# A written order for VectorE, ScalarE and TensorE in the opening of a float32 attention and GEGLU kernel, without waits between neighbours

## The chip, the cores and the metric

The kernel runs on one core of one Trainium2 chip. The metric is device time in microseconds (us) of one execution. One profiled execution gives the span, the instructions of each engine, their waits and the DMA transfers; its own device time stands beside its span below.

## The reference

All tensors are float32. From the same x (2048 tokens, 512 channels) two branches are computed and mixed by a gate for each token:

```python
x = A_x
g = _sigmoid((x * gate_w).sum(-1, keepdims=True))
a = _A_ref(x, A_wqkv, A_wo)
b = _B_ref(x, B_w_gate, B_w_up, B_w_down)
return g * a + (1 - g) * b
```

Branch A is attention with 32 heads of 16 channels. Each token looks at itself and at the seven tokens 2, 4, ... 14 places before it, then comes the product with wo. Branch B is `(gelu(x @ w_gate) * (x @ w_up)) @ w_down` with 1792 hidden channels.

## The kernel before

**Precision.** TensorE reads fp32r, a rounded float32. So each operand is split into a high part (`hi`, the rounded value, made by a ScalarE activation `AF.Copy`) and a low part (`lo = raw - hi`, made by a VectorE subtraction). A product of two operands is three matmuls: hi x hi, lo x hi, hi x lo. The helper `split` (line 81) issues both, hi first.

**Two halves of tokens.** Tokens are worked on in two halves (`par` 0 and 1) of 1024, each as eight tiles of 128 (`jj`), four to a block. Each half has a projection to K and Q, one to V and the gate, an FFN of 14 chunks (`ffn`, `gate_up`, `down`) and four units of attention on VectorE (`scores`, `softmax`, `mix`), spread between the matmuls of the FFN by `pull`. A scheduler sorts what the program leaves open, from priorities and an estimate of times; the result is a fixed sequence of instructions for each engine.

**The opening** is `start()` (from line 834 on). It makes K and Q of the first half, as a 2 x 2 block product in seven block products (Strassen's scheme in Winograd's form) in place of eight. The operands are a11, a12, a21, a22 of x (512 tokens or channels each) and b11, b12, b21, b22 of the weights, and their sums:

- x: s1 = a21 + a22, s2 = s1 - a11, s4 = a12 - s2, s3 = a11 - a21. In the code `q[kc][0..3]` are a11, a12, a21, a22 of one K chunk (kc 0 or 1), and `s12` holds s1 and then s2.
- weights, in place: t1 = b12 - b11, t2 = b22 - t1, t3 = b22 - b12, t4 = b21 - t2.

`block(ps, a, w, ...)` issues the 24 matmuls of one block product: four tiles, two K chunks, three matmuls each. The order is a11 x b11 (into the banks `U`, acc0 to acc3), a12 x b21 (into `V_`, four banks of tag p, seeded with a copy of U), s1 x t1 (`Z_`, the same four banks again), s2 x t2 (onto U), s4 x b22 (onto Z_), s3 x t3 (onto U), a22 x t4 (onto U). Between them ScalarE evicts: `put` writes K and Q of the first two units from V_ and in the end from U, `p5` is the copy of Z_ after s1 x t1, `u2` that of U after s2 x t2. `join` adds such a copy to a bank on VectorE and stores K and Q of the other two units over SP's queue.

The first half block (tile 0 of a11 x b11) runs on the first 128 tokens that land. Then come two fillers, and the first chunk for the other three tiles.

**What sets the order.** `row` (class `Row`, line 815) wraps VectorE: each instruction that it issues gets a dependency of class Sync on the one before, so a semaphore wait on its predecessor. `mm` and the fillers are chained through `paced` and `LAST` in the same way on TensorE. ScalarE has no written order in the opening; the scheduler places its roundings and evictions. SP's queue carries the loads, in the order that the scheduler gives it: x, weights, then the stores of K and Q, the loads of the FFN (`fetch`, `fetch_d`) and of the V weights (`vs`).

**Where tiles come free.** `RAW` (the FFN weights of a chunk) takes the two `raw` tiles that hold x, `XR`, so chunk 0 and 1 are loaded when the last low part has been read from them. The V weights' raw tiles are four of tag c, two of which held parts of b22 and t3. The weights b11, b21, b12 and b22 lie in the tiles `prod`, `v` and `tb` that attention uses later.

**After the opening**: `sums(f)` forms the four sums of the FFN weights of a chunk (the FFN uses the same seven products, line 497), `parts(i)` splits them into the tiles g0 and g1, and `ffn(0)` starts with the V projection of tile 0 and 1 among its products (line 189).

Of the kernel before, what the change touches and what calls it, by code (L numbers as in the profile page):

```python
# [37 lines left out]
BT = 4  # L38
# [9 lines left out]
def tile_gated_mix(ctx: ExitStack, tc: tile.TileContext, xt, wqkv, wff, wo, out):  # L48
# [308 lines left out]
    def after(ins, other):  # L357

        tc.add_manual_dep(ins.ins, other.ins.name, mybir.DependencyInfo(mybir.DependencyClass.Sync,
                          mybir.DependencyReason.SCHED_ONLY), reason="pace")  # L360

    def paced(ins):
        after(ins, LAST[-1])
# [452 lines left out]
    class Row:  # L816

        last = None

        def __getattr__(self, name):  # L820
            def do(*args, **kw):
                ins = getattr(nc.vector, name)(*args, **kw)
                if Row.last is not None:
                    after(ins, Row.last)
                Row.last = ins
                return ins
            return do

    row = Row()
# [5 lines left out]
    def start():  # L835
# [5 lines left out]
        for kc in range(2):  # L841
            XR[kc] = tl("raw")

# [7 lines left out]
        def quarters(t):  # L851
            return [t[:, i * 512:(i + 1) * 512] for i in range(4)]

        def operand(name, src, rooms_):
            KW[name] = [tuple(rooms_[2 * k:2 * k + 2]) for k in range(2)]
            for k in range(2):
                split(row, *KW[name][k], src[:, k * 512:(k + 1) * 512])
# [3 lines left out]

        def rooms_of(tag, n, w=512):
            t = tl(tag, F32R)
            return [t[:, i * w:i * w + 512] for i in range(n)]
# [15 lines left out]
        KW["b11"] = [tuple(g1a[2 * k:2 * k + 2]) for k in range(2)]  # L880
        split_x(0, 0, 0, ((0, P),), row.tensor_copy, row)
        split(row, *KW["b11"][0], b11[:, :512])
        split_x(0, 0, 0, ((P, 512 - P),), row.tensor_copy, row)
        split_x(0, 0, 1, eng=row)
        split(row, *KW["b11"][1], b11[:, 512:])
        U = [bank(f"acc{t}") for t in range(BT)]

        def mm(ps, t, a, w, first=False, last=False):
            ins = nc.tensor.matmul(ps, a[:, t * P:(t + 1) * P], w, start=first, stop=last, skip_group_check=True)  # L889
            paced(ins)  # L890
            LAST[:] = [ins]

        (xh, xl), (wh, wl) = X[0, 0, 0], KW["b11"][0]
# [3 lines left out]
        for _ in range(FILLERS):  # L897
            ins = nc.tensor.matmul(U[-1][:, :P], warm[:, :P], warm[:, :P], start=True, stop=True)
            paced(ins)
            LAST[:] = [ins]  # L900
# [6 lines left out]
        def block(ps, a, w, first, then, kcs=(0, 1)):  # L907
            for t in range(BT):
                for kc in kcs:
                    ah, al = XOP[a, kc]  # L910
                    wh, wl = KW[w][kc]
                    for n, (a_, w_) in enumerate(((ah, wh), (al, wh), (ah, wl))):
                        mm(ps[t], t, a_, w_, first and kc == 0 and n == 0, kc == 1 and n == 2)
                if then:
                    then(t)

        for n, blk, k in (("a11", 0, 0), ("a12", 0, 2), ("a22", 1, 2)):
            for kc in range(2):
                XOP[n, kc] = X[0, blk, kc + k]
        V_ = []  # L920

        def seed(t):
            V_.append(bank("p"))
            nc.scalar.activation(V_[t], U[t], AF.Copy)

        block(U, "a11", "b11", False, seed, (1,))
        split_x(0, 0, 2, eng=row)
        split_x(0, 0, 3, eng=row)
        operand("b21", b21, g1b)

        def put(jj, ps):
            take_first(ps, jj, lambda o, i: nc.scalar.activation(o, i, AF.Copy))

        block(V_, "a12", "b21", False, lambda t: put(t, V_[t]))
# [7 lines left out]
        q = [quarters(XR[kc]) for kc in range(2)]  # L942
# [3 lines left out]
        for kc in range(2):  # L946
# [5 lines left out]
        p5, u2 = [], []  # L952

        def keep_p5(t):
            p5.append(tl("hh")[:, :512])
            nc.scalar.activation(p5[t], Z_[t], AF.Copy)

        def keep_u2(t):
            u2.append(tl("hl")[:, :512])
            nc.scalar.activation(u2[t], U[t], AF.Copy)  # L960
# [7 lines left out]
        block(Z_, "s1", "t1", True, keep_p5)  # L968
        for kc in range(2):
            sub(s12[kc], s12[kc], q[kc][0])  # L970
        for kc in range(2):
            split(row, *XOP["s2", kc], s12[kc])
        sub(b11, b22, b11)
        operand("t2", b11, d[4:])
        block(U, "s2", "t2", False, keep_u2)
        for kc in range(2):
            sub(q[kc][1], q[kc][1], s12[kc])
        for kc in range(2):
            split(row, *XOP["s4", kc], q[kc][1])
        tl("g0")  # L980
        operand("b22", b22, rooms_of("g0", 3, WA) + rooms_of("c", 1))
        for kc in range(2):
            sub(q[kc][0], q[kc][0], q[kc][2])
        for kc in range(2):
            split(row, *XOP["s3", kc], q[kc][0])
        for kc in (2, 3, 0, 1):
            split_x(0, 1, kc, copy=held, eng=row)
# [3 lines left out]
        sub(b12, b22, b12)  # L991
        operand("t3", b12, [r for _ in range(3) for r in rooms_of("s", 1)] + rooms_of("c", 1))
        block(Z_, "s4", "b22", False, lambda t: join(t, Z_[t], u2[t]))
        sub(b21, b21, b11)
        operand("t4", b21, g1b)
        block(U, "s3", "t3", False, lambda t: join(BT + t, U[t], p5[t]))
        vs = []
        for kc in range(KC):
            t = tl("d", F32R)
            hi, lo = WC[1, kc] = t[:, :WQ + CU], t[:, VL:VL + WQ + CU]  # L1000
# [3 lines left out]
            vs.append((hi, lo, raw[:, :WQ + CU]))  # L1004
# [8 lines left out]
        def parts(i):  # L1013
            n = len(GROUPS[i]) * QW
            w = tl(f"g{i}", F32R)
            hi, lo = w[:, :n], w[:, n:2 * n]
            for k, op in enumerate(GROUPS[i]):
                WG[0, op] = hi[:, k * QW:(k + 1) * QW], lo[:, k * QW:(k + 1) * QW]
            split(row, hi, lo, RAW[0][:, (0, 4)[i] * QW:][:, :n])
            if not i:  # L1020
                KEEP[0] = w[:, :2 * n]

        sums(0)
# [71 lines left out]
```

## Time and profile before

| | us |
|---|---|
| median of 3 runs | 619.38 (619.29 to 619.82) |
| profiled execution, device time | 619.28 |
| its span | 617.5 |
| TensorE busy | 601.1 (97%) |
| VectorE busy | 532.2 (86%) |
| ScalarE busy | 386.7 (63%) |
| GpSimd busy | 79.1 (13%) |
| mean DMA rate | 212 GB/s |

The page lists 8208 instructions, 2802 of them matmuls. Matmuls are pipelined: one of 512 columns is shown as 0.39 us long while the next starts much sooner, so a busy share near 100% does not say that matmuls follow each other without a gap; starts and counts do. In rows of the order of time the columns are start, length, engine, line, operation, output<-inputs, shape and count, and in brackets the idle time before and what ended it. An engine name with a q is its queue, where waits stand and transfers are issued. Line 822 is the call inside `row`, line 889 the matmul inside `mm`, line 86 the rounding in `split`.

### The profile page before, as it was taken

The page shows a single profiled execution, that of the slowest core. Times are in us where ns is not written, and L with a number is a line of the kernel's source. Part 1 is how long each engine was busy: PE and PEld are TensorE (multiplying, and loading weights), DVE is VectorE, ACT ScalarE, POOL GpSimd, SP SyncE. Part 2 cuts the span into 40 slices and gives each one's busy share as a digit, 9 for nine tenths or more (in the row PEclk, how much of TensorE's full clock was granted, in tenths as well). Part 3 has the DMA queues.
Part 4 walks back from the last instruction along what each step waited for, and adds up shares of the span by engine and source line. Part 5 has one row for each costly group of instructions (what it writes and reads, how often), then busy time and mean ns, then how long its engine had stood idle before and what let it go on. Part 6 is the DMA issues. An engine that isn't in the chain of part 4 may idle for free.

```text
span 617.5 us, 8208 instructions
## 1 busy us (share of the span) xinstructions
PE 601.1 (97%) x2802; PEld 499.5 (81%) x2802; DVE 532.2 (86%) x611; ACT 386.7 (63%) x651; POOL 79.1 (13%) x106
## 2 busy tenths in 40 slices
PE   8879999999999999999999999999999999999996
PEld 6557998778888888888899888888888888888885
DVE  5788698999898978799997998899799879999882
ACT  5635556587677866868374438566865676674722
POOL 0500101121121221201100001111110111101200
PEclk9989999999999999999999999999999999999998
DMA  7146989698889889795669979686777896937614
GB/s 272 46 136 196 280 249 281 175 285 231 216 239 296 224 231 283 198 253 170 232 192 285 308 222 283 184 239 162 239 182 217 199 258 144 279 107 201 90 40 165
DMA packets 84584, 131.04 MB, mean 212 GB/s; under 512 B 7999, under 2 KB 52159, under 8 KB 84542
## 3 DMA queue, kind: packets, MB, share of 16 engines
q1 hardware_dynamic: 63310, 94.27, 46.8%
q0 software_dynamic: 12096, 31.40, 26.7%
q10 hardware_dynamic: 9136, 4.85, 2.6%
q8 instruction: 22, 0.36, 0.2%
q14 instruction: 20, 0.16, 0.1%
HBM read 67.18 MB, written 36.77 MB: 168 GB/s over the span
## 4 chain that ended last, share of the span: by engine, by line
PE 82%; DVE 7%; DMA 5%; issue 3%; ACT 2%; SPq 0%; DVEq 0%; POOL 0%; ACTq 0%; POOLq 0%
PE p L497 37%; PE p L537 11%; PE acc L537 11%; PE acc L189 9%; PE p L763 5%; PE acc L889 2%; PE p L889 2%; DVE lg L301 2%; PE p L189 2%; PE acc L763 2%; DVE prod L298 1%; DMA prod<-wqkv 1%; DMA kq<-qs 1%; DMA g<-raw 1%; DMA kq<-kq 1%
## 5 line engine op out<-in xcount | busy, mean ns | idle before, releaser
L497 PE MATMUL p<-S,g 128*128 128x512 f32 x672 | 166.0, 389 | 0.0
L497 PEld LDWEIGHTS p<-S,g 128*128 128x128 f32 x672 | 125.9, 188 | 26.2
L497 PE MATMUL p<-A,g 128*128 128x512 f32 x504 | 126.5, 390 | 0.6 <-DMA g<-raw 0.6
L497 PEld LDWEIGHTS p<-A,g 128*128 128x128 f32 x504 | 94.2, 188 | 20.9 <-DMA g<-raw 1.4
L298 DVE TENSOR_TENSOR prod<-kq 128x2048 f32<-128x2048 f32 x32 | 73.2, 2287 | 14.1 <-DMA kq<-kq 5.3
L455 POOL DMA_DIRECT2D g<-raw x40 | 34.7, 867 | 344.1 <-ACT g L454 131.5
L336 DVE TENSOR_TENSOR prod<-v,lg 128x2048 f32<-128x2048 f32 x32 | 73.0, 2281 | 6.5 <-PE acc L537 2.1
L301 DVE TENSOR_REDUCE lg<-prod 128x128 f32<-128x2048 f32 x32 | 73.1, 2283 | 0.3
L537 PE MATMUL p<-d,hh 128*128 128x512 f32 x224 | 68.1, 389 | 0.0
L537 PE MATMUL acc<-d,hh 128*128 128x512 f32 x224 | 58.6, 390 | 1.2 <-ACT hh L513 1.2
L537 PEld LDWEIGHTS acc<-d,hh 128*128 128x128 f32 x224 | 42.0, 188 | 10.3 <-ACT hh L513 1.6
L537 PEld LDWEIGHTS p<-d,hh 128*128 128x128 f32 x224 | 42.0, 188 | 8.7
L459 ACT ACTIVATE g<-raw 128x1024 fp32r<-128x1024 f32 (+1 forms) x40 | 39.5, 990 | 13.2 <-PE p L497 13.0
L502 ACT ACTIVATE s<-p 128x512 f32<-128x512 f32 x56 | 33.0, 593 | 20.9 <-PE p L497 20.7
L514 DVE TENSOR_TENSOR hl<-c,hh 128x512 fp32r<-128x512 f32 x56 | 38.3, 685 | 7.8 <-ACT hh L513 7.3
L454 ACT ACTIVATE g<-raw 128x1024 fp32r<-128x1024 f32 (+1 forms) x40 | 39.3, 984 | 7.9 <-DVE raw L436 6.7
L507 DVE TENSOR_TENSOR c<-p,s 128x512 f32<-128x512 f32 x56 | 37.9, 684 | 6.6 <-PE p L497 6.5
L537 PE MATMUL p<-d,hl 128*128 128x512 f32 x112 | 42.8, 389 | 0.0
L513 ACT ACTIVATE hh<-c 128x512 fp32r<-128x512 f32 x56 | 35.0, 626 | 10.6 <-DVE c L511 10.3
L511 DVE TENSOR_TENSOR c<-c 128x512 f32<-128x512 f32 x56 | 38.3, 684 | 3.3 <-ACT c L602 2.7
L340 DVE TENSOR_TENSOR prod<-prod 128x1024 f32<-128x1024 f32 x32 | 39.1, 1221 | 0.5
L550 ACT ACTIVATE rt<-p 128x512 f32<-128x512 f32 x48 | 28.2, 592 | 14.6 <-PE p L537 14.1
(190 smaller groups left out, 921.7 us busy)
## 6 DMA issues: line engine op xcount, KB each, us to landing
g<-raw POOLq DMA_DIRECT2D x27, 512.0 KB, 6.3
raw<-wff SPq DMA_DIRECT2D x42, 256.0 KB, 4.0
ws<-g SPq DMA_DIRECT2D x14, 768.0 KB, 5.5
g<-ws SPq DMA_DIRECT2D x14, 768.0 KB, 5.5
r<-wff SPq DMA_DIRECT2D x28, 256.0 KB, 4.2
d<-r POOLq DMA_DIRECT2D x26, 256.0 KB, 6.3
g<-raw POOLq DMA_DIRECT2D x13, 384.0 KB, 5.7
v<-vs SPq DMA_DIRECT2D x8, 512.0 KB, 6.4
```

The lines of the kernel that those rows point to most:

```text
L189: LAST[:] = [nc.tensor.matmul(ps[:, :cn], a[:, t], w[:, c0:c0 + cn], start=(kc == 0 and n == 0), stop=(kc == KC - 1 and n == 2))]
L298: paced(nc.vector.tensor_tensor(prod, spans(k, jj), q[:, jj:jj + 2, None, :].to_broadcast([P, 2, W, UC]), op=OP.mult))
L301: nc.vector.tensor_reduce(two_of(lg, jj), prod.rearrange("p j w (h d) -> p (j w) h d", d=DH), axis=AX.X, op=OP.add)
L336: paced(nc.vector.tensor_tensor(prod.rearrange("p j w (h d) -> p (j w) h d", d=DH), spans(v, jj).rearrange("p j w (h d) -> p j w h d", d=D ...
L340: nc.vector.tensor_tensor(prod[:, :, :4], prod[:, :, :4], prod[:, :, 4:], op=OP.add)
L454: nc.scalar.activation(lo, raw, AF.Copy, scale=-1.0)
L459: ins = nc.scalar.activation(hi, raw, AF.Copy)
L497: LAST[:] = [nc.tensor.matmul(ps, w_, a_, start=(start and kc == 0 and n == 0), stop=(kc == 1 and n == 2), skip_group_check=True)]
L511: nc.vector.tensor_tensor(ge, ge, up, op=OP.mult)
L514: nc.vector.tensor_tensor(hl_, ge, hh_.bitcast(F32), op=OP.subtract)
L537: LAST[:] = [nc.tensor.matmul(pp, a[:, ts], w, start=(i == 0 and n == 0 and gr == 0), stop=(i == 1 and n == 2), skip_group_check=True)]
L763: LAST[:] = [nc.tensor.matmul(pa, a, b, start=(first and n == 0), stop=(last and n == 2), skip_group_check=True)]
```

## The change

Four things, all up to chunk 0 of the FFN.

1. `Row` becomes a class for any engine, with three of it: `row` (VectorE), `act` (ScalarE) and `mms` (TensorE). The dependency of an instruction on the one before has class NoSync: it fixes the order and adds no semaphore wait. Waits that data ask for stay.
2. `split` is taken apart into `hi(n, k)` on `act` and `lo(n, k)` on `row`, so that high and low parts can be placed one by one. Operands have names (`OP_`, `SRC`).
3. Orders are written anew. The sum of the next weights stands ahead of the low parts of the former operand. Evictions on ScalarE stand between the roundings. The joins of U go ahead of a22 x t4, those of Z_ behind it. The high and low parts of a22 and a21 come behind t3's.
4. The raw tiles of the third and fourth chunk of the V weights are the freed tiles of b22 and b12 in place of two of tag c. They are loaded ahead of the FFN's chunk 0.

The matmuls, their order on TensorE in the opening and their number stay.

```diff
-    def after(ins, other):
+    def after(ins, other, cls=mybir.DependencyClass.Sync):
...
     class Row:
-        last = None
+        def __init__(self, eng):
+            self.eng, self.last = eng, None
+
+        def add(self, ins):
+            if self.last is not None:
+                after(ins, self.last, mybir.DependencyClass.NoSync)
+            self.last = ins
+            return ins
...
-    row = Row()
+    row, act, mms = Row(nc.vector), Row(nc.scalar), Row(nc.tensor)
...
+        def hi(n, k):
+            act.activation(OP_[n, k][0], SRC[n, k], AF.Copy)
+
+        def lo(n, k):
+            h, l = OP_[n, k]
+            row.tensor_tensor(l, SRC[n, k], h.bitcast(F32), op=OP.subtract)
...
-        split_x(0, 0, 0, ((0, P),), row.tensor_copy, row)
-        split(row, *KW["b11"][0], b11[:, :512])
-        split_x(0, 0, 0, ((P, 512 - P),), row.tensor_copy, row)
-        split_x(0, 0, 1, eng=row)
-        split(row, *KW["b11"][1], b11[:, 512:])
+        tokens(0, P)
+        hi("b11", 0)
+        lo("b11", 0)
+        tokens(P, 512)
+        hi("a11", 1)
+        hi("b11", 1)
+        lo("a11", 1)
+        lo("b11", 1)
...
-        split_x(0, 0, 2, eng=row)
-        split_x(0, 0, 3, eng=row)
-        operand("b21", b21, g1b)
+        for n, k in (("b21", 0), ("a12", 0), ("b21", 1), ("a12", 1)):
+            hi(n, k)
+            lo(n, k)
...
-        for kc in range(2):
-            row.tensor_tensor(s12[kc], q[kc][2], q[kc][3], op=OP.add)
-        for kc in range(2):
-            split(row, *XOP["s1", kc], s12[kc])
-        sub(b11, b12, b11)
-        operand("t1", b11, d[:4])
+        for k in range(2):
+            row.tensor_tensor(s12[k], q[k][2], q[k][3], op=OP.add)
+        put(0, V_[0])
+        both(hi, "s1")
+        put(1, V_[1])
+        sub(b11, b12, b11)
+        for k in range(2):
+            hi("t1", k)
+            lo("s1", k)
+            lo("t1", k)
+        put(2, V_[2])
+        put(3, V_[3])
...
+        block(Z_, "s4", "b22", False)
+        sub(b12, b22, b12)
+        both(lo, "s3")
+        both(hi, "t3")
+        both(lo, "t3")
+        block(U, "s3", "t3", False)
+
+        both(hi, "a22", "a21")
+        both(lo, "a22", "a21")
         for f in range(2):
             fetch(f)
         fetch_d(0)
-        sub(b12, b22, b12)
-        operand("t3", b12, [r for _ in range(3) for r in rooms_of("s", 1)] + rooms_of("c", 1))
-        block(Z_, "s4", "b22", False, lambda t: join(t, Z_[t], u2[t]))
-        sub(b21, b21, b11)
-        operand("t4", b21, g1b)
-        block(U, "s3", "t3", False, lambda t: join(BT + t, U[t], p5[t]))
...
-            raw = tl("c")
+            raw = tl("c") if kc < 2 else (b22, b12)[kc - 2]
...
+        sub(b21, b21, b11)
+        join(BT, U[0], p5[0])
+        both(hi, "t4")
+        both(lo, "t4")
+        for t in range(1, BT):
+            join(BT + t, U[t], p5[t])
+        block(U, "a22", "t4", False)
...
+        for t in range(BT):
+            join(t, Z_[t], u2[t])
+        both(hi, "v")
         sums(0)
         parts(0)
-        for x in vs:
-            split(row, *x)
+        both(lo, "v")
+        put(BT, U[0])
+        for kc in (2, 3):
+            hi("v", kc)
+            lo("v", kc)
+        put(BT + 1, U[1])
         parts(1)
+        put(BT + 2, U[2])
+        put(BT + 3, U[3])
         sums(1)
-        block(U, "a22", "t4", False, lambda t: put(BT + t, U[t]))
```

More of the change, by code (lines that the diff above doesn't have):

```diff
@@ L816, in tile_gated_mix @@
     class Row:
-        last = None
-        def __getattr__(self, name):
[L821 to L827, printed above, removed]
-    row = Row()
+        def __init__(self, eng):
[5 more added lines that the diff above has]
+            return ins
+        def __getattr__(self, name):
+            return lambda *args, **kw: self.add(getattr(self.eng, name)(*args, **kw))
+    row, act, mms = Row(nc.vector), Row(nc.scalar), Row(nc.tensor)
     def stage(name, shape):
@@ L842, in start @@
             XR[kc] = tl("raw")
+        q = [[XR[kc][:, i * 512:(i + 1) * 512] for i in range(4)] for kc in range(2)]
         def load_w(dst, hh, half, cols=slice(0, 1024), queue=nc.sync):
@@ L849, in load_x @@
             nc.sync.dma_start(XR[kc % 2][:, o:o + n], xt[blk, :, kc, a:a + n])
[L851 to L857, printed above, removed]
-        def sub(o, a, b):
-            row.tensor_tensor(o, a, b, op=OP.subtract)
         def rooms_of(tag, n, w=512):
@@ L966, in join @@
             nc.sync.dma_start(rows(QS[0, 1], jj), two[:, 1])
[L968 to L972, printed above, removed]
-        sub(b11, b22, b11)
[L974 to L987, printed above, removed]
+        for k in range(2):
+            sub(s12[k], s12[k], q[k][0])
+        out_of(p5[0], Z_[0])
+        both(hi, "s2")
+        out_of(p5[1], Z_[1])
+        sub(b11, b22, b11)
+        for k in range(2):
+            hi("t2", k)
+            lo("s2", k)
+            lo("t2", k)
+        out_of(p5[2], Z_[2])
+        out_of(p5[3], Z_[3])
+        block(U, "s2", "t2", False)
+        for k in range(2):
+            sub(q[k][1], q[k][1], s12[k])
+        both(hi, "s4")
+        out_of(u2[0], U[0])
+        both(lo, "s4")
+        both(hi, "b22")
+        out_of(u2[1], U[1])
+        both(lo, "b22")
+        for k in range(2):
+            sub(q[k][0], q[k][0], q[k][2])
+        out_of(u2[2], U[2])
+        both(hi, "s3")
+        out_of(u2[3], U[3])
+        block(Z_, "s4", "b22", False)
[6 more added lines that the diff above has]
+        both(lo, "a22", "a21")
         for f in range(2):
```

100 lines of the change are left out of this document (62 added, 38 removed).

## The prediction, made before the changed kernel ran

> **What bounds the kernel now.** I read the shares of the chain that ended last, then what TensorE waited for, then busy time by stretch, then the instructions of the first 60 us in order of time.
>
> ```profile
> PE 82%; DVE 7%; DMA 5%; issue 3%; ACT 2%; SPq 0%; DVEq 0%; POOL 0%; ACTq 0%; POOLq 0%
> ...
> 147.84 2.72 PE p L497 x12
> ```
>
> TensorE holds 82% of the chain, and twelve of its 512-wide matmuls take 2.72 us there: 0.227 us each. That is the unit of everything below.
>
> ```profile
> PE acc L889 <- ACT s L86: 3.8, 1, 3.8
> PE p L889 <- ACT d L86: 1.3, 1, 1.3
> PE acc L889 <- ACT d L86: 1.2, 1, 1.2
> PE acc L537 <- ACT hh L513: 1.2, 1, 1.2
> ...
> PE acc L889 <- DVE hh L822: 0.8, 1, 0.8
> PE p L497 <- DMA g<-raw: 0.6, 1, 0.6
> ```
>
> Of TensorE's six longest waits behind data, four stand at line 889, the opening; only two (1.2 and 0.6) come later. By stretch (busy us of TensorE, its weight loads, VectorE, ScalarE, GpSimd, each with its count; granted clock; DMA share; GB/s):
>
> ```profile
> 40.00:50.00 10.00, 7.70 (x23) 6.04 (x24) 7.91 (x11) 3.57 (x6) 0.00 (x0) 0.66 0.88 263
> 110.00:120.00 10.00, 8.80 (x39) 6.86 (x39) 10.00 (x10) 5.24 (x10) 1.71 (x2) 1.00 0.59 133
> 150.00:300.00 150.00, 150.00 (x664) 124.24 (x662) 132.74 (x163) 110.87 (x176) 25.48 (x32) 1.00 0.87 241
> ```
>
> From 150 to 300 us TensorE has no idle at all, while VectorE has 17 us of it. In the opening TensorE idles, and in 40 to 50 us its granted clock is only 0.66. So what is saved on TensorE's path before 57 us should reach the end, unless VectorE, full from 110 to 120, does not come along.
>
> The opening itself:
>
> ```profile
> 6.52 3.00 PE L889 MATMUL acc<-g,A 128*128 128x512 f32 x11 [0.32 <-DVE A L822]
> 9.74 2.54 PE L889 MATMUL acc<-g,A 128*128 128x512 f32 x10 [0.22 <-DVE g L822]
> 13.06 5.33 PE L889 MATMUL p<-g,A 128*128 128x512 f32 x22 [0.33 <-DVE g L822]
> 17.06 1.23 DVE L822 TENSOR_TENSOR prod<-v,prod 128x1024 f32<-128x1024 f32 x1
> 18.97 1.15 ACT L86 ACTIVATE d<-prod 128x512 fp32r<-128x512 f32 x2
> 19.65 6.12 PE L889 MATMUL p<-d,S 128*128 128x512 f32 x24 [1.26 <-ACT d L86]
> 26.98 6.13 PE L889 MATMUL acc<-d,S 128*128 128x512 f32 x24 [1.21 <-ACT d L86]
> 40.36 1.23 DVE L822 TENSOR_TENSOR v<-tb,v 128x1024 f32<-128x1024 f32 x1
> 41.62 1.15 ACT L86 ACTIVATE s<-v 128x512 fp32r<-128x512 f32 x2 [4.76 <-DVE v L822]
> 42.30 2.50 PE L889 MATMUL acc<-s,S 128*128 128x512 f32 x5 [3.76 <-ACT s L86]
> 51.34 5.69 PE L889 MATMUL acc<-g,A 128*128 128x512 f32 x24 [0.81 <-DVE hh L822]
> ```
>
> Each time the pattern is the same: VectorE forms a weight sum late (17.06, 40.36), ScalarE rounds it (18.97, 41.62), TensorE starts 0.05 to 0.7 us behind. After the 3.76 us wait it also runs slowly: five matmuls in 2.50 us, where 22 took 5.33 before, about half the pace.
>
> From 6.52 to the last block's end stand 9 + 12 + 6 x 24 = 165 matmuls, 165 x 0.227 = 37.4 us. They end at 51.34 + 24 x 0.227 = 56.78, after 50.3 us. **The opening loses 12.9 us**, and that is the most that the change can win there.
>
> **The change part by part.** *TensorE's and ScalarE's orders.* TensorE's opening matmuls keep their order and carried no waits on neighbours before; nothing is gained by that alone. ScalarE's order is now written: evictions between roundings.
>
> ```profile
> 6.33 0.63 ACT L86 ACTIVATE g<-prod 128x512 fp32r<-128x512 f32 x1 [2.06 <-DMA prod<-wqkv]
> ```
>
> One rounding is 0.63 us, and the two neighbours at 18.97 took 1.15, so 0.52 from start to start.
>
> *VectorE without waits between neighbours.* The price of such a wait:
>
> ```profile
> 13.76 1.42 DVE L822 TENSOR_TENSOR r<-raw 128x512 f32<-128x512 f32 x2
> 102.52 1.28 DVE L507 TENSOR_TENSOR c<-p,s 128x512 f32<-128x512 f32 x2
> ```
>
> Two of 0.69 us take 1.42 with the wait (start to start 0.73) and 1.28 without one (0.60). So 0.13 us for each of VectorE's some 40 chained instructions, 5 us on VectorE, which reaches TensorE only where VectorE is late. I take 0.60 and keep 0.73 as the other end. Beside this, the Trainium skill ("VectorE: DVE Perf Modes", "The DRAIN you can't avoid") says that a semaphore between Vector instructions costs nothing extra, because the pipe drains anyway; by it the pitch would stay at 0.73, the first rival below. These two rows disagree with it.
>
> *Sums ahead of low parts.* VectorE's queue, followed by hand with 0.60 for 512 columns and 1.13 for 1024, ScalarE's with 0.52, and 0.04 us from one engine to the next. The second weight quarters land when they did:
>
> ```profile
> 7.60 0.33 SPq L845 DMA_DIRECT2D v<-wqkv  x1
> v<-wqkv SPq DMA_DIRECT2D x1, 512.0 KB, 6.4
> raw<-wff SPq DMA_DIRECT2D x42, 256.0 KB, 4.0
> ```
>
> - Start: the first nine matmuls at 6.46. The other half of a11 and b11 is now rounded in this order (7.6 and 8.1), so that b11's low part comes at 9.6, hardly before the 9.74 of the old row, where the same part ended the wait. Without it TensorE would be there at 6.46 + 11 x 0.227 = 8.95; these 0.7 us stay lost. The first two blocks end 10 matmuls later, at 11.9.
> - a12 x b21: the operands are split alternately, the last low part at 12.0, needed at 12.8. The 0.33 us wait at 13.06 goes; the block runs 11.9 to 17.3.
> - s1 x t1: the sum for t1 starts when v lands, 7.60 + 6.4 = 14.0, and ends at 15.2; the first rounding follows the second eviction, 15.5 to 16.2. TensorE is free at 17.3, so 1.1 us to spare; block 17.3 to 22.8.
> - s2 x t2: t2's sum ends at 20.5, its first rounding at 21.6, needed at 22.8.
> - s4 x b22: last rounding at 26.8, last low part at 27.7, needed from 28.2.
> - s3 x t3: the sum stands ahead of s3's low parts and of all of a22 and a21 (in the old trace it came behind eight low parts, at 40.36). It ends at 30.0, rounding at 31.2, needed at 33.7. The 3.8 us wait goes, and with it the slow matmuls behind it.
> - a22 x t4: sum done at 35.9, roundings at 37.1, first join (which frees the bank) at 36.5, needed at 39.1. Block 39.1 to 44.5.
>
> TensorE thus ends the opening at 44.54 instead of 56.78: **12.2 us earlier**. The margins, 1.1 to 2.5 us, are the cover of the low parts and roundings that I cost at nothing; where one is used up, TensorE waits for the excess only.
>
> *The joins and loads moved.* s4's joins go behind the last block's, and the V weights' loads ahead of the first FFN chunk's on SP's queue, two of them into the freed tiles of b22 and b12. They are smaller than the FFN's loads of 4.0 us; issued at 30.0 to 32.5, they are in by 36.5. The FFN loads go out when a21's low parts are done, 34.2 to 36, and are in by 40. Neither is waited for: VectorE reaches the chunk's sums only at 42.3, behind the eight joins.
>
> ```profile
> 53.62 1.61 DVE L822 TENSOR_TENSOR raw<-raw 128x512 f32<-128x512 f32 x3
> 62.29 1.97 SPq L276 DMA_DIRECT2D kq<-kq  x2
> 63.49 0.86 ACT L454 ACTIVATE g<-raw 128x768 fp32r<-128x768 f32 x1
> 68.01 2.29 DVE L298 TENSOR_TENSOR prod<-kq 128x2048 f32<-128x2048 f32 x1 [5.31 <-DMA kq<-kq]
> ```
>
> *The hand-over to chunk 0.* Sums done at 42.3 + 1.6 = 43.9, rounding (768 columns, 0.86) at 44.8: TensorE, free at 44.5, waits 0.3 us. The eviction of the last block's first bank, which the value matmuls need, now stands behind this rounding on ScalarE, at 45.3, and the low part of the chunk's weights ends at 45.8: 0.3 us more. **0.6 us given back.**
>
> *Attention's start.* SP reaches the copy inside kq behind the evictions' stores, two kept sums and two loads at about 52.1 instead of 62.29, 10.2 us earlier, so VectorE's first product moves from 68.01 to about 57.8. Attention gains 1.4 us less than TensorE. Is that waited for? At the end:
>
> ```profile
> 607.26 0.69 DVE L87 TENSOR_TENSOR hl<-raw,hh 128x512 fp32r<-128x512 f32 x1 [1.41 <-ACT hh L86]
> 609.04 1.98 PE L763 MATMUL p<-S,hh 128*128 128x512 f32 x8
> ```
>
> The last unit's high part is ready at 607.2 and used in the run at 609.04, its low part some 2 us before its use: between 1 and 2 us of slack, and VectorE's idle time between absorbs some. Of the 1.4 us I charge half, 0.7; the ends are 0 and 1.4.
>
> **Sum**: -12.2 + 0.6 + 0.7 = -10.9, say -11. The profiled execution took 619.28 us (span 617.5), 0.1 from the median of 619.38, so 619.3 - 10.9 = **608.4 us**.
>
> **The rivals.**
> 1. *Taking the waits away saves nothing on VectorE* (0.73 stays). The same walk gives t3's rounding at 32.5 and t4's at 38.7, still in time, but the chunk's sums at 47.0 instead of 43.9: TensorE waits 3.2 us more, 611.6. Against it: the two rows above. 7%.
> 2. *VectorE's queue stays the limit up to 130 us.* It is full at 110 to 120 us, and TensorE's late waits (1.2 and 0.6) lie there. If attention gets ahead by less than computed, say 8 us, TensorE is held there: 611 to 613. For it: VectorE's 10.00; against it: its 17 us of idle from 150 to 300. 13%.
> 3. *The late waits go too*, since the new order puts chunk 1's hidden work ahead of unit 1's first product: 1.8 us better and no lag charged, 605 to 607. 12%.
> 4. *Slower.* In the new order the V rows of unit 0 are loaded ahead of K and Q of unit 1 on SP:
>
> ```profile
> 90.00:100.00 10.00, 10.00 (x45) 8.20 (x45) 7.54 (x13) 9.00 (x15) 0.85 (x1) 1.00 0.93 254
> ...
> 88.42 0.43 SPq L279 DMA_DIRECT2D kq<-qs  x1
> 95.18 2.29 DVE L298 TENSOR_TENSOR prod<-kq 128x2048 f32<-128x2048 f32 x1 [1.81 <-DMA kq<-qs]
> ```
>
> VectorE already waited for that transfer. V is 512 + 448 KB, at the 254 GB/s of that time 3.9 us, and it must itself wait for the last V stores. If this transfer lands no earlier than before but 4 to 6 us later, everything behind VectorE's fifth product, the hidden parts that TensorE needs among it, comes later than in the old run: 619.3 + 4 to 6, so 623 to 625. It decides if Q of unit 1 lands after 95 us; by my walk it lands near 88, with 7 us of FFN work for VectorE in front of it. 6%.
> 5. *No effect* (waits not gone, or the opening wholly hidden): the built order shows the waits gone, and TensorE's row is the chain's. 2%.
>
> **How the numbers follow.** Forecast (607 to 610) 60%, rivals 7, 13, 12, 6 and 2. The range 605 to 613 takes in the first three rivals and the ends of the pitch and the lag, and leaves out some 15%. A measurement of this kernel tells 0.2%, 1.2 us, from no change. Faster: 60 + 7 + 13 + 12 = 92, less 1 for a rival 2 that goes further: 0.91; same 0.03; slower 0.06.
>
> **What would show it.** TensorE's waits at line 828 (the new helper) should hold no entry over 1 us; the granted clock should be 1.00 from 10 us on; the a22 x t4 block should end near 44.5 and chunk 0's first matmul start within 0.5 us of it; VectorE's neighbours in the opening should be 0.60 apart; the first product should start near 58; the stretches after 150 us should show TensorE full as before. The prediction is wrong if a block waits for a rounding queued behind an eviction, if the first FFN load lands after 42 us, or if TensorE's waits after 60 us grow past 2 us.

## The result, and the profile after

| | before | after |
|---|---|---|
| median, us | 619.98 (619.01 to 622.95, 20 runs) | 611.80 (609.59 to 620.06, 20 runs) |
| ratio, 95% interval | | 0.9884 (0.9859 to 0.9908) |
| profiled execution, us | 619.28 | 612.35 |
| its span, us | 617.5 | 610.6 |

The change makes the kernel faster by 8.2 us in the medians, 6.9 us between the two profiled executions, where 10.9 were forecast. The runs after spread widely: 15 of the 20 lie between 609.6 and 614.2 at a mean granted clock of 0.995 or more, five between 617.5 and 620.1 at 0.989 to 0.992; none of these five was profiled, and what made them longer stays open.

The opening went as forecast. In order of time on TensorE, from the second block on:

```profile
11.87 5.60 PE L828 MATMUL p<-g,A 128*128 128x512 f32 x24
17.30 5.60 PE L828 MATMUL p<-d,S 128*128 128x512 f32 x24
22.75 5.60 PE L828 MATMUL acc<-d,S 128*128 128x512 f32 x24
28.18 1.30 PE L828 MATMUL p<-g,S 128*128 128x512 f32 x5
...
33.62 1.30 PE L828 MATMUL acc<-s,S 128*128 128x512 f32 x5
...
39.06 5.60 PE L828 MATMUL acc<-g,A 128*128 128x512 f32 x24
...
44.51 0.62 PE L497 MATMUL p<-A,g 128*128 128x512 f32 x2
```

Each block starts 5.43 to 5.45 us after the one before, 24 x 0.227, and no row has a bracket: nothing is waited for. The forecast starts were 11.9, 17.3, 22.8, 28.2, 33.7 and 39.1. Chunk 0 (line 497) begins at 44.51, 0.01 us after the last block would end. Before it began at 57.34, behind four matmuls of the V projection, which came first there:

```profile
56.87 0.64 PE L189 MATMUL acc<-d,A 128*128 128x258 f32 x4
```

So TensorE left the opening 12.4 us earlier (56.87 to 44.51).

TensorE's longest waits behind data, whole run (engine, line, releaser: us in total, times, longest), without the one at the very start of the program:

```profile
PE p L497 <- DMA g<-raw: 2.4, 3, 1.3
PE p L497 <- DVE c L507: 2.0, 1, 2.0
...
PE p L497 <- ACT s L502: 1.0, 1, 1.0
PE acc L828 <- DVE A L828: 0.5, 1, 0.5
```

The four long entries of the opening are gone; line 828 keeps 0.5. In their place the FFN's line 497 waits 5.4 us, where the old view had 1.8 behind the opening. This is the mark that the prediction named as its failure (over 2 us after 60 us). The rows themselves:

```profile
85.52 1.66 PE L497 MATMUL p<-S,g 128*128 128x512 f32 x6 [1.02 <-ACT s L502]
...
108.58 1.66 PE L497 MATMUL p<-A,g 128*128 128x512 f32 x6 [2.01 <-DVE c L507]
...
124.23 2.57 PE L497 MATMUL p<-A,g 128*128 128x512 f32 x10 [1.30 <-DMA g<-raw]
...
201.14 1.20 PE L497 MATMUL p<-A,g 128*128 128x512 f32 x4 [0.96 <-DMA g<-raw]
```

They begin 41 us behind the hand-over and end at 201; so part of what the opening won is paid back here, not at its own end. 3.0 us stand behind VectorE and ScalarE (`c`, `s`), 2.4 behind weights that a DMA brings (`g<-raw`). The granted clock (seventh figure, ahead of DMA share and GB/s) is full in both stretches:

```profile
10.00:58.00 48.00, 47.99 (x246) 40.75 (x245) 37.41 (x58) 31.81 (x68) 10.15 (x18) 1.00 0.65 194
58.00:605.00 547.00, 541.33 (x2524) 451.37 (x2523) 483.17 (x542) 351.18 (x576) 67.76 (x82) 1.00 0.79 216
```

Why VectorE comes late is seen at attention's first product (line 298) and on SP's queue. In order of time, a load of the opening, some of the queue's longer issues from 49 us on (start, time that the queue spent on the issue), and VectorE's first product:

```profile
34.67 0.46 SPq L426 DMA_DIRECT2D raw<-wff  x1
...
49.20 1.90 SPq L472 DMA_DIRECT2D ws<-g  x1
...
53.69 1.02 SPq L425 DMA_DIRECT2D raw<-wff  x1
...
54.81 1.26 SPq L466 DMA_DIRECT2D ws<-raw  x1
56.12 1.32 SPq L426 DMA_DIRECT2D raw<-wff  x1
57.49 2.88 SPq L276 DMA_DIRECT2D kq<-kq  x2
...
64.44 2.29 DVE L298 TENSOR_TENSOR prod<-kq 128x2048 f32<-128x2048 f32 x1 [14.08 <-DMA kq<-kq]
```

The copy inside kq was forecast at 52.1 and came at 57.49. What stands ahead of it from 46.44 on is what the prediction counted (the evictions' stores, eight here, two kept sums and two loads) and one kept sum more. These 13 issues took 11.0 us, since five of them were long: a load of line 426 held the queue for 0.46 us at 34.67 and for 1.32 at 56.12. From 54 us on the DMA engines were full (last three figures: clock, DMA share, GB/s):

```profile
54.00:58.00 4.00, 3.99 (x31) 3.66 (x30) 0.00 (x0) 0.72 (x3) 0.00 (x0) 1.00 1.10 219
```

That this is what lengthens an issue is not shown: the longest, 1.90 us at 49.20, stands where the DMA share is 0.71 (46 to 50 us) and 0.65 (50 to 54), and the load at 34.67 took 0.46 at a share of 0.90 (34 to 36).

VectorE's busy time, ahead of the first (x0), is 0.00: it idles for the 14.08 us of the bracket above, while TensorE goes on. TensorE reached chunk 0 12.8 us earlier (57.34 to 44.51), attention only 3.6 us (68.01 to 64.44).

### The profile page after: what moved, and what is told of

Read it like the earlier page. It is cut to its first block, busy times and chain, and to the rows that moved or that the text cites. A ratio compares the mean times of both kernels' runs of the same rounds, so it can differ in the third digit from the quotient of the medians.

```text
span 610.6 us, 8186 instructions
## 1 busy us (share of the span) xinstructions
PE 598.4 (98%) x2802; PEld 498.0 (82%) x2802; DVE 526.0 (86%) x611; ACT 388.7 (64%) x653; POOL 79.2 (13%) x106
## 4 chain that ended last, share of the span: by engine, by line
PE 79%; DMA 8%; issue 7%; ACT 2%; DVE 1%; SPq 1%; ACTq 1%; POOL 0%; POOLq 0%; DVEq 0%
PE p L497 35%; PE acc L537 11%; PE p L537 11%; PE acc L189 9%; PE p L763 5%; DMA g<-raw 4%; PE p L828 3%; PE acc L828 2%; PE p L189 2%; PE acc L763 2%; DMA raw<-wff 1%; DMA prod<-wqkv 1%; DMA ws<-g 1%; ACTq L215 1%; DMA vs<-c 1%
## 5 line engine op out<-in xcount | busy, mean ns | idle before, releaser
L497 PE MATMUL p<-A,g 128*128 128x512 f32 x504 | 128.2, 391 | 4.4 <-DMA g<-raw 2.4
L537 PE MATMUL acc<-d,hh 128*128 128x512 f32 x224 | 61.3, 390 | 0.2 <-DMA d<-r 0.2
L513 ACT ACTIVATE hh<-c 128x512 fp32r<-128x512 f32 x56 | 35.0, 626 | 10.2 <-DVE c L511 10.0
L550 ACT ACTIVATE rt<-p 128x512 f32<-128x512 f32 x48 | 28.2, 593 | 17.4 <-PE p L537 16.9
```

Of the source, the lines that this page charges most:

```text
L497: LAST[:] = [nc.tensor.matmul(ps, w_, a_, start=(start and kc == 0 and n == 0), stop=(kc == 1 and n == 2), skip_group_check=True)]
L537: LAST[:] = [nc.tensor.matmul(pp, a[:, ts], w, start=(i == 0 and n == 0 and gr == 0), stop=(i == 1 and n == 2), skip_group_check=True)]
```

## The experiments

Two theories. **A**: the copy inside kq lands late, attention runs behind the FFN, and from 85 us on VectorE's and ScalarE's queues, longer by what was left undone, make TensorE wait. **B**: the late waits belong to the new fixed order and its transfers, whatever the copy does. Each kernel was timed in five rounds beside the kernel before on the same chip. There were three groups, each on another chip (medians of before 619.66 to 620.2); the changed kernel again and the two that move the copy in the new order share one. Where a kernel's program is a line shorter, the line numbers in the rows are one lower.

### The changed kernel again

> The changed kernel once more, beside the others on the same chip. Theory A (lag): its late TensorE waits (7 us from 57 us on) come from VectorE's attention, which starts at 64.4 us behind the copy inside kq. Theory B (order): they come from the new static order and from transfers after 80 us, whenever attention starts. Both expect 610 to 613 us as the median against 619 to 621 of the kernel before, a ratio of 0.985 to 0.990, and VectorE idle for some 14 us before its first product. Seen so far: 5 of 20 runs at 617 to 620 us with a granted clock of 0.99; if a profile falls on one of these, a stretch at half clock should be found in it.

609.59 us (608.97 to 610.89), ratio 0.9836 (0.9821 to 0.9851). The first product stood at 64.87. TensorE's late waits were 2.0, 1.0 and 1.0, so the pattern of the first trace repeats; the time is 2.2 us below the first median, which sets how far two measurements of this kernel can lie apart.

### The copy ahead on SP's queue, and on GpSimd's

```diff
-        load_kq(0, 0)
         yield from scores(0, 0)
...
         put(BT + 3, U[3])
+        load_kq(0, 0)
         sums(1)
```

This alone is the first kernel. The second also issues the copy from the other engine:

```diff
-                nc.sync.dma_start(k[a:b, :NP - 1], k[a - 1:b - 1, NP:])
+                nc.gpsimd.dma_start(k[a:b, :NP - 1], k[a - 1:b - 1, NP:])
```

> The copy inside kq stands ahead of the chunk loads and of the second kept sum on SP's queue, everything else of the change is kept. It can go out when the last store of K and Q is issued, about 53.5 us, so VectorE's first product should start at 58 to 60 in place of 64.4. Theory A: TensorE's late waits shrink with the lag, about 2 us better than the changed kernel, 609 to 610. Theory B: no better, 611 to 612.5.

> The same copy issued from GpSimd's queue, which stands idle there, so that it waits only for the last eviction at 48.4: landed by 53 to 55, first product at 53 to 55. Theory A: the lag is gone (TensorE 12.2 us and attention 13 us earlier than before the change), late waits under 2.5 us as before the change, 607 to 608.5. Theory B: 611 to 613, late waits still 5 us or more.

On SP's queue: 613.95 us (612.78 to 614.99), ratio 0.9903 (0.9889 to 0.9918). In order of time:

```profile
53.60 2.83 SPq L276 DMA_DIRECT2D kq<-kq  x2
...
62.54 2.29 DVE L298 TENSOR_TENSOR prod<-kq 128x2048 f32<-128x2048 f32 x1 [12.45 <-DMA kq<-kq]
```

The place in the program moved the issue by 3.9 us and the product by 1.9 only: the stores of K and Q are still ahead, and the transfer itself took longer, 8.9 us from issue to product against 7.0. The time is 4.4 us longer than that of the changed kernel on the same chip (609.59), though the product came earlier: against A, and longer than B's 611 to 612.5. The edit also changed the built order: in the two traces another matmul stands at 442 of TensorE's 2802 places, another instruction at 183 of VectorE's 611.

From GpSimd: **606.47 us** (605.71 to 607.69), ratio 0.9787 (0.9773 to 0.98), the fastest of all kernels tried. In order of time:

```profile
48.36 1.09 POOL L276 DMA_DIRECT2D kq<-kq  x2 [22.31 <-ACT hl L827]
...
54.56 2.29 DVE L298 TENSOR_TENSOR prod<-kq 128x2048 f32<-128x2048 f32 x1 [4.33 <-DMA kq<-kq]
```

GpSimd issues the copy when its data are there, with nothing else in front. TensorE's longest waits, of this kernel:

```profile
PE p L496 <- ACT rt L549: 0.7, 1, 0.7
PE acc L827 <- DVE A L827: 0.7, 1, 0.7
PE p L496 <- DMA g<-raw: 0.4, 1, 0.4
PE acc L536 <- DVE d L87: 0.2, 1, 0.2
```

And of the one with the copy on SP's queue:

```profile
PE p L496 <- ACT s L501: 3.5, 2, 2.7
PE acc L189 <- ACT z L219: 2.3, 2, 1.6
PE p L496 <- DMA g<-raw: 2.1, 2, 1.8
...
PE p L496 <- ACT rt L549: 0.7, 1, 0.7
```

The two kernels differ in the engine that issues the copy. The product comes 8.0 us earlier, 8.6 us of late waits shrink to 1.3 (line 827 is the opening), and the time falls by 7.5 us. Their built orders differ too, but late: by lines, tiles and shapes in the traces, the first 665 matmuls of TensorE are the same (up to 142.5 and 135.1 us), and VectorE's first 157 instructions (up to 147.8 and 140.7). So the same matmul can be looked up in both, on SP's queue and from GpSimd:

```profile
128.08 1.19 PE L496 MATMUL p<-A,g 128*128 128x512 f32 x4 [1.80 <-DMA g<-raw]
```

```profile
120.57 1.21 PE L496 MATMUL p<-A,g 128*128 128x512 f32 x4 [0.39 <-DMA g<-raw]
```

At chunk 0 the kernel with the copy on GpSimd was 0.1 us behind (44.38 for 44.24); here it is 7.5 ahead, all of the gain. About 1.9 us of it arise up to a wait at 73.9 us where ScalarE's order differs by one rounding. And the copy's leaving SP's queue also lets the two FFN loads behind it out 3.7 us earlier (54.19 and 56.02 for 57.84 and 59.78). So it is shown that the copy on SP's queue costs several microseconds in this order, as A has it; attention's start and the earlier loads are not told apart by any run.

The Trainium skill ("DMA: Bandwidth & Descriptors", "Issuing engines are not separate DMA queues") says that issuing from several engines saves only the issuing engine's own time, "usually small relative to the DMA itself". The first half agrees: from issue to product are 7.0 us in the changed kernel (57.49 to 64.44) and 6.2 here. The second half does not hold here: the issue came 9.1 us earlier (48.36 for 57.49), more than the whole transfer.

### The same copy in the old kernel

Same two edits, with the call ahead of the last line of `start()` of the kernel before.

> The kernel before, opening untouched, but the copy inside kq issued early from GpSimd's queue, as in kq_pool. First product near 63 in place of 68.0. If attention's start alone sets the end in the old kernel too: 5 us, 615. If the old kernel was bound by TensorE's opening and attention only costs its late waits there (1.4 + 0.8 us): 618 to 619.5. kq_pool gained 13.7 over the old kernel; the difference to this run is then what the opening is worth once attention is out of the way.

619.55 us (618.24 to 621.28), ratio 0.9999 (0.9986 to 1.0012). The first product, in order of time:

```profile
63.29 2.29 DVE L298 TENSOR_TENSOR prod<-kq 128x2048 f32<-128x2048 f32 x1 [2.49 <-PE acc L189]
```

4.7 us earlier than the old kernel's 68.01 and worth nothing: attention has room there, and its first product waits for TensorE. In the new order the copy's queue was worth 7.5, so the copy became a limit only when the opening got shorter.

### The waits on VectorE put back

```diff
-                after(ins, self.last, mybir.DependencyClass.NoSync)
+                cls = mybir.DependencyClass.Sync if self.eng is nc.vector else mybir.DependencyClass.NoSync
+                after(ins, self.last, cls)
```

Once with the copy where the change has it, and once with the copy from GpSimd.

> The changed kernel with its new orders, but VectorE's neighbours chained by semaphore waits as before (ScalarE and TensorE without). If a wait costs 0.13 us: neighbours 0.73 apart in the opening, no TensorE wait up to a22 x t4, but the sums of chunk 0 end 2.5 to 3.2 us later and so does chunk 0's first matmul (47 to 48 us in place of 44.5). If the rest of the run then follows TensorE: 614 to 615. If attention's start (64 us, set by the copy inside kq) is the limit anyway, part is hidden: 612 to 613. If waits cost nothing (pitch stays 0.60): 611.8.

> kq_pool (new orders, early copy) with VectorE's semaphore waits put back. Seen so far: where VectorE's first product starts 11 us or less behind the end of TensorE's opening, the late TensorE waits stay under 3 us (before 2.4, kq_pool 2.2, old_kq_pool 2.8), where it starts 13 us or more behind, they are 5 to 13. Theory A: with attention early, each part costs what it costs in the opening and no more. Here chunk 0 starts 5.4 us later (49.9 against 44.5), so 606.5 + 5.4 = 612 (610.5 to 613). Theory B (the static order decides by chance): no relation, anything from 606 to 620, as dve_waits without the early copy gave 619.8.

With the late copy 619.83 us (618.33 to 621.37), ratio 0.9993 (0.9982 to 1.0004): all of the gain is gone, 4.8 us above the upper end expected; eight matmuls at half pace from 97 us on (last section) are a part of it, some 1.6 us. With the early copy 611.88 us (611.59 to 612.04), ratio 0.9872 (0.9859 to 0.9885), as expected. VectorE and TensorE in order of time, early copy:

```profile
37.22 1.49 DVE L828 TENSOR_TENSOR rt<-raw,rt 128x512 fp32r<-128x512 f32 x2
...
40.91 2.00 PE L828 MATMUL acc<-g,A 128*128 128x512 f32 x6 [0.74 <-DVE hh L828]
...
43.21 4.38 PE L828 MATMUL acc<-g,A 128*128 128x512 f32 x18 [0.29 <-DVE hh L828]
...
49.76 0.83 PE L496 MATMUL p<-A,g 128*128 128x512 f32 x2 [2.17 <-ACT g L828]
```

A pair of low parts takes 1.49 where the same pair of the changed kernel takes 1.29 (below): 0.80 from start to start instead of 0.60. The delay adds up until the last block waits for its joins and chunk 0 for the rounding of its sums. Chunk 0 starts at 49.76, 5.4 us later than with the early copy and no waits (44.38), and the time is 5.4 us longer. So here a microsecond at chunk 0's start is one at the end.

The changed kernel's pair, in order of time:

```profile
33.51 1.29 DVE L828 TENSOR_TENSOR rt<-raw,rt 128x512 fp32r<-128x512 f32 x2
```

### Only the waits taken away, in the old order

```diff
                 if Row.last is not None:
-                    after(ins, Row.last)
+                    after(ins, Row.last, mybir.DependencyClass.NoSync)
```

`after` gets the class as an argument, as in the change; everything else is the kernel before. Again once with each place of the copy.

> The kernel before with its own orders, but VectorE's chain without semaphore waits (class NoSync). With dve_waits this makes the four corners of order and waits. VectorE gains 0.12 to 0.2 us on each chained instruction: the sum for t3 should start near 38 in place of 40.36, so the 3.8 us wait shrinks to 1.5 to 2 and TensorE should stay at full clock behind it. If parts add up (order alone gave nothing, both gave 10.6): 610 to 612. If order and waits need each other: 614 to 617, of it 2.4 us from the clock.

> The old orders, VectorE's chain without waits, and the early copy. Theory A: the opening ends at 52.0 in place of the old 56.8 (a t3 wait of 3.0 us and 2 us of half clock stay), so 4.8 us better than the old kernel with the early copy (619.6): 614 to 616, late waits under 3 us. Theory B: 618 to 623, as without the early copy (622.5).

Late copy: 622.47 us (621.56 to 623.54), ratio 1.005 (1.0036 to 1.0063), slower than before. Early copy: 619.61 (618.3 to 623.49), ratio 1.0004 (0.999 to 1.0018). TensorE in order of time, late copy:

```profile
38.65 1.93 PE L889 MATMUL acc<-s,S 128*128 128x512 f32 x5 [2.87 <-ACT s L86]
...
46.54 5.73 PE L889 MATMUL acc<-g,A 128*128 128x512 f32 x24 [0.25 <-DVE hh L822]
```

The last block starts 4.8 us earlier than in the old trace (46.54 for 51.34), though t3's wait of 2.87 us stays, and none of it reaches the end. The late copy's time lies above both values expected, the early copy's in B's range. Behind chunk 0 TensorE waits for 6.9 us, and for 6.3 with the early copy, where the old kernel waits for 1.8; both have matmuls at half pace behind some of these waits. That the early copy did not keep the 4.8 us counts against A as the only cause.

### The sum behind the low parts again

```diff
         block(Z_, "s4", "b22", False)
-        sub(b12, b22, b12)
         both(lo, "s3")
+        both(hi, "a22", "a21")
+        both(lo, "a22", "a21")
+        sub(b12, b22, b12)
         both(hi, "t3")
         both(lo, "t3")
         block(U, "s3", "t3", False)
-        both(hi, "a22", "a21")
-        both(lo, "a22", "a21")
```

> The changed kernel with one step of its order undone: the sum for t3 again behind the low parts of s3, a22 and a21, waits still taken away. By the margins of the prediction VectorE forms it at 32.7 to 33.9 and TensorE, free at 33.6, waits 1.0 us for the rounding: no slow clock, chunk 0 within 1 us of the changed kernel's 44.5; 609.5 to 612 (the rest of the order shifts by 1 to 2 us either way). Rival: the place of the sum is what the 3.8 us wait and the slow clock behind it hung on; then both come back and the time is 614 or more.

> kq_pool with the sum for t3 put back behind the low parts of s3, a22 and a21. Theory A: its own 1.3 us wait in the opening and little more, 607.5 to 609, late waits under 3 us and no half clock. Theory B: 612 to 620, as sum_late without the early copy (619.6).

Late copy: 619.55 us (617.95 to 621.33), ratio 0.9995 (0.9983 to 1.0006). The rival's 3.8 us wait did not come back in the opening (1.1 us, chunk 0 at 45.68); what is lost lies behind it. Early copy: 611.09 (609.92 to 612.47), ratio 0.986 (0.9841 to 0.9878), 2.1 us above the upper end that A expected and below B's range. TensorE in order of time, early copy:

```profile
34.83 1.69 PE L827 MATMUL acc<-s,S 128*128 128x512 f32 x5 [1.11 <-ACT s L827]
...
60.99 1.70 PE L189 MATMUL acc<-d,A 128*128 128x258 f32 x12 [1.71 <-ACT z L219]
...
63.76 1.69 PE L189 MATMUL acc<-d,A 128*128 128x256 f32 x12 [1.07 <-ACT hl L211]
```

Directly the place of the sum is worth 1.8 us: the wait of 1.11 and short gaps among the next matmuls (five in 1.69), so that chunk 0 starts at 46.15 for 44.38. Most of the rest of the 4.6 us against the kernel with the early copy alone is in two waits of the V projection at 61 and 64 us, which that kernel does not have.

### All V weights in tag c

```diff
-            raw = tl("c") if kc < 2 else (b22, b12)[kc - 2]
+            raw = tl("c")
```

> The changed kernel with part 4 undone: all four raw tiles of the V weights are of tag c again, so the third and fourth load wait for TensorE's s4 x b22 and s3 x t3. By the prediction nobody waits for these loads: chunk 0 at 44.5, 609.5 to 611.5. Rival: they hold up SP's queue, the copy inside kq and attention's start come 1 to 4 us later than 64.9, and the time follows: 611 to 614.

> kq_pool with all four raw tiles of the V weights of tag c. Theory A: the opening did not wait for them in v_in_c either (no wait over 0.15 us between 7 and 63 us), so 606 to 608. Theory B: 610 to 616, as v_in_c without the early copy (615.5).

Late copy: 615.48 us (613.46 to 615.84), ratio 0.9927 (0.9912 to 0.9942). Early copy: 615.6 (612.71 to 616.77), ratio 0.9925 (0.9906 to 0.9945), where A expected 606 to 608. Chunk 0 starts on time in both (44.16 and 44.51), and the early copy brings the first product to 52.44, the earliest of all. Still VectorE and then TensorE wait, in order of time, early copy (its profiled execution took 612.71, the shortest of its six):

```profile
82.50 0.17 DVE L241 TENSOR_SCALAR en<-en 128x8 f32<-128x8 f32 x1 [3.49 <-ACT en L240]
...
88.70 1.66 PE L496 MATMUL p<-S,g 128*128 128x512 f32 x6 [2.58 <-ACT s L501]
...
126.70 1.19 PE L496 MATMUL p<-A,g 128*128 128x512 f32 x4 [2.56 <-DMA g<-raw]
```

This speaks for B: late waits though attention started well ahead. But its lead does not last. ScalarE waits for stores of V (2.34 us at 76.43, 2.40 at 79.28; 1.46 and 0.59 in the kernel with the early copy alone), VectorE waits behind it, and the first product of unit 1 comes at 84.57, later than the 83.45 of that kernel. Why four tiles of tag c bring this is open; it was not tried further.

### All kernels in one table

From each profiled execution: the start of chunk 0's first matmul, the start of attention's first product, the difference, and the rest of the span behind chunk 0's start.

| kernel | chunk 0 | first product | attention behind | rest |
|---|---|---|---|---|
| before | 57.34 | 68.01 | 10.7 | 560.2 |
| after | 44.51 | 64.44 | 19.9 | 566.1 |
| after, again | 44.51 | 64.87 | 20.4 | 563.9 |
| copy ahead on SP | 44.24 | 62.54 | 18.3 | 568.2 |
| copy on GpSimd | 44.38 | 54.56 | 10.2 | 559.9 |
| old, copy on GpSimd | 57.16 | 63.29 | 6.1 | 560.9 |
| waits back | 49.94 | 67.22 | 17.3 | 568.6 |
| waits back, GpSimd | 49.76 | 59.29 | 9.5 | 560.3 |
| old without waits | 52.34 | 65.13 | 12.8 | 568.6 |
| old without waits, GpSimd | 52.63 | 59.70 | 7.1 | 566.4 |
| sum late | 45.68 | 64.81 | 19.1 | 571.2 |
| sum late, GpSimd | 46.15 | 57.97 | 11.8 | 563.5 |
| V in c | 44.16 | 65.63 | 21.5 | 569.4 |
| V in c, GpSimd | 44.51 | 52.44 | 7.9 | 566.4 |

In the kernels of the old order two or four matmuls of the V projection stand ahead of chunk 0's first, which makes their rest look shorter by up to 0.5 us.

The rest is 560 to 561 in four kernels, all with attention at most 10.7 us behind. With attention 11.8 us behind it is 563.5, with 12.8 us or more 564 to 571, never 560. In these kernels the short rest goes only with near attention, but two with 7 to 8 us still have 566: near attention does not suffice. Two kernels with attention 18 to 20 us behind differ by 4.3 us in the rest (the copy ahead on SP, and the changed kernel again), so the lag alone does not set it.

## Why the prediction came out as it did

The kernel is faster, and the forecast of 608.4 lies 3.4 us below the median; the two measured medians of the changed kernel, 611.80 and 609.59, both lie between the forecast and its upper end of 613. That the second lies only 1.2 us off is in part luck: one term of the sum was far too small, another did not come, and the opening gave slightly more. By the terms of the sum, in the profiled executions (span 617.5 to 610.6, -6.9):

**Opening, -12.2: right.** The blocks started within 0.1 us of the hand-worked times, and TensorE left the opening 12.4 us earlier. That VectorE's pitch falls to 0.60 was right (1.29 for a pair), and so the first rival fell. Its price was too low: it gave chunk 0 3.2 us of waiting with 0.73 for all neighbours, and putting the waits back cost 5.4, with 0.80 for the low parts. The Trainium skill's rule that a semaphore between Vector instructions costs nothing extra ("VectorE: DVE Perf Modes", "The DRAIN you can't avoid") is thus contradicted by time too: 611.88 against 606.47 us.

**Hand-over, +0.6: did not come.** Chunk 0 began without a wait. The prediction let ScalarE round the chunk's weights behind all three sums, at 43.9; these 768 columns were rounded from 43.44 on, ahead of the third sum's end at 43.87:

```profile
43.44 0.85 ACT L828 ACTIVATE g<-raw 128x768 fp32r<-128x768 f32 x1 [5.21 <-DVE raw L828]
```

**Attention's start and its lag, +0.7: the step that failed.** The prediction wrote that the copy inside kq is issued "at about 52.1 instead of 62.29, 10.2 us earlier", and the product moves to 57.8; it was issued at 57.49 and the product came at 64.44, 3.6 us earlier. The prediction gave the queue's issues ahead of the copy their old lengths; in the new trace they are 13 and took 11.0 us, five of them 0.9 to 1.9 us each, and from issue to product went 7.0 us where 5.7 did before. Attention's lag behind chunk 0, 19.9 us instead of the 12.7 forecast, was then priced by slack at the end of the kernel, where a unit's high and low parts are used. It was paid between 85 and 201 us, by TensorE behind `c`, `s` and the chunks' weights. From the end of the opening on, the execution grew by 5.5 us, in place of 0.7: -12.4 + 5.5 = -6.9, the measured difference. TensorE's waits account for it: counted from start to start against the usual 0.227 and 0.12 us, it loses 8.0 us behind 60 us, and 2.3 before the change. In the second execution the growth is 3.3 us.

How much of the term is the copy's lateness is not settled for the changed kernel itself. With the copy from GpSimd the rest is 559.9, as short as before, and the time 606.47; that is 5.3 us below the first median and 3.1 below the second, on the same chip as the latter. But in that kernel another matmul stands at 434 of TensorE's 2802 places, another instruction at 183 of VectorE's 611, and the same copy ahead on SP's queue, in nearly that order, took 4.4 us more than the changed kernel. What is shown is the pair on SP's and GpSimd's queue: 7.4 us arise there while TensorE's and VectorE's orders are the same.

**Rivals.** The second came about: attention ahead by less (3.6 us; the rival took 8), TensorE held before 130 us (and once more at 201), 611 to 613 by the first median. It had 13% and was the right mechanism, except that VectorE was first held by the copy, idle for 14 us, and not by its own queue. The third came only in the variant with the early copy, which lies in its 605 to 607. The fourth did not: the wait for Q of unit 1 ended at 93.97, short of the 95 from which it decides, though much later than the 88 of the walk:

```profile
93.97 2.29 DVE L298 TENSOR_TENSOR prod<-kq 128x2048 f32<-128x2048 f32 x1 [1.54 <-DMA kq<-qs]
```

**The parts.** That the change as a whole is needed is shown: new order with waits 619.83, old order without them 622.47, both 611.80. Each alone gains nothing here. With the early copy the new order gains 7.7 us by itself (619.55 to 611.88), the missing waits nothing in the old order (619.55 to 619.61) and 5.4 us in the new one (611.88 to 606.47).

**Open.** What makes the late waits in the kernels with V in tag c and in the old order without waits, where attention starts near; what lengthens an issue on SP's queue; and how the changed kernel's 5.5 us divide between the late copy and the new order.

## What to carry to other kernels

When a stage on the bounding engine gets shorter, work through the in-order queues that feed the next stage with the lengths that their issues will have in the new neighbourhood, not with the old ones: the issue of a small copy behind stores and loads moved by 4.8 us (62.29 to 57.49) where the stage moved by 12.4. A small transfer that releases an engine belongs on a queue with nothing in front of it, and its worth has to be tried together with the change that makes it the limit: in the old kernel it was worth 0, in the new order 7.5 us against the same copy on SP's queue and 3 to 5 against the changed kernel. The parts of such a change do not add up, so a part that measures as nothing alone is not shown to be useless.

## What was not expected of the hardware

A wait of about 2 us on TensorE can be followed by some three microseconds of matmuls at half pace, and the length of the wait does not decide it. Behind 60 us it came at seven places in five of the kernels, after waits of 1.82 to 3.10 us, and did not come after waits of 2.01, 2.56, 2.58 and 2.70. The old order without waits and with the copy from GpSimd, in order of time, and its stretches (granted clock in the seventh figure):

```profile
162.53 4.10 PE L496 MATMUL p<-A,g 128*128 128x512 f32 x10 [2.04 <-DMA g<-raw]
```

```profile
162.00:164.00 2.00, 1.48 (x4) 1.19 (x5) 2.00 (x3) 0.33 (x1) 0.00 (x0) 0.61 1.03 236
164.00:166.00 2.00, 2.00 (x6) 1.58 (x5) 1.89 (x1) 0.58 (x1) 0.00 (x0) 0.53 1.08 237
```

Ten matmuls took 4.10 us; in the changed kernel's row at 124.23 ten took 2.57. The row at 108.58 of the changed kernel has the same wait (2.01), and the V-in-c row at 88.70 a longer one (2.58), and both go on at full pace (six matmuls in 1.66). The stretch behind the latter:

```profile
88.00:90.00 2.00, 1.30 (x6) 1.08 (x7) 2.00 (x3) 2.00 (x5) 0.00 (x0) 1.00 1.09 315
```

The Trainium skill ("TensorE: Matmul & The Clock Gate", "Part 1: The HAM clock gate") gives about 3.4 us of an idle window for the drop to half rate and says that the window runs freely. The half rate agrees; the waits here are shorter than that figure. That the window's position decides would fit, and no run here tells it apart.
